# Two unused 96-byte tiles that move every large tile to a multiple of 128 bytes in its partition

## The chip, the core and the metric

The kernel runs on one core of one Trainium2 chip. A core has a matrix engine (TensorE, in the profile PE for the matrix multiplications and PEld for the loads of their stationary operand), VectorE (DVE), ScalarE (ACT), GpSimd (POOL), a queue engine that issues transfers (SP), and 16 DMA engines. They share an on-chip memory (SBUF) of 128 partitions; a tile has the same byte address in each of its partitions. TensorE writes its sums to another memory, PSUM, of 8 banks. The metric is the device time of one execution in microseconds; lower is better. Before the change the median of three runs is 2217.54 us (2216.56 to 2222.09).

## The reference

Three parts follow each other. `B, H, S, D` is 4, 8, 768, 48; the token matrix is 3072 by 384.

```python
for t in range(S):                                   # delta rule, 32 heads
    kt, vt, bt = k_n[:, :, t], v[:, :, t], beta[:, :, t, None]
    y[:, :, t] = einsum('bhd,bhde->bhe', q[:, :, t], state)
    v_old = einsum('bhde,bhd->bhe', state, kt)
    state = state + bt * einsum('bhd,bhe->bhde', kt, vt - v_old)
x = y.transpose(0, 2, 1, 3).reshape(3072, 384)
P = exp(x @ w_gate - max)                            # 8 experts
for _ in range(8):
    P /= P.sum(1) + 1e-9;  P /= P.sum(0) + 1e-9;  P *= N / E
out = sum(P[:, e] * (relu(x @ w1[e]) @ w2[e]) for e in range(8))   # 384 -> 1024 -> 384
a, b = out @ m2_w1, out @ m2_w2                      # 384 -> 1024, twice
return ((a * b) @ w3) @ w_out                        # 1024 -> 1024 -> 384
```

## The kernel before, in words

All large matrix products are done in the type fp32r, with each operand split in a high and a low part, so one product is three matmuls: high times high, high times low, low times high. A matmul loads a 128 x 128 stationary operand (its weights, read from SBUF by PEld) and streams a moving operand of 128 partitions by 512, 384 or 256 columns from SBUF past it. In the profile a matmul is written `b<-x,y`: `b` is a PSUM bank, `x` and `y` its two SBUF operands in alphabetical order, so the name alone doesn't say which of them moves; this section does.

Stage 1, until about 510 us, is the attention, in 12 chunks (`prep_k`, `invert`, `tt_make`, `prep_q`, `seq`), with expert 0 beside it (`e0`): there the moving operand is `xr` or `hA`, the weights are slots of `wA`, and a matmul has 256 columns.

Stage 2, 510 to 1878 us, is experts 1 to 7 (`unit`, line 975 on), in three passes over the tokens, with two halves of each expert: 42 units. A unit first computes the hidden layer: the weights are in `wA` or `wS`, the moving operand is one of nine token forms, of which three are in `xr` and six in `xT`, 512 columns. ScalarE and VectorE put relu of the result, split in high and low, into one of nine slots, seven in `hB` and two in `hA`. The second half of the unit has these slots as its moving operand, again 512 columns, and its weights in `wA`: six sums of 12 matmuls each. VectorE scales each sum (`tmp`), and GpSimd adds it to `acc`. Weights of the next unit come from DRAM by two large DMAs a pair (`load_pair`); VectorE, ScalarE and GpSimd also convert the last layer's weights there (`convert`).

Stage 3, from 1878 us (`phase_c`), first multiplies `w3` by `w_out` (384 columns, moving `wA`, weights `wS`), then takes the tokens in six chunks of 512. Each chunk has 144 matmuls of 512 columns, whose weights are in `xT` and whose moving operand is the split token chunk. That chunk lies in `xr` or in `wS`, by turns (`x2`, with the same code for both); then 96 matmuls of 384 columns follow with the weights in `hB` and `hA` and the moving operand in `wA`.

The order of all instructions is fixed when the kernel is built: a planner (`Plan.order`) takes each operation's priority and assumed cost and simulates the engines. Addresses don't enter it.

SBUF tiles are given out by `open`, which opens a pool on the left (low addresses, growing up) or on the right (high addresses, growing down) and places its tiles one after the other, each rounded up to 32 bytes. Pools close in the order of a stack, and what is opened later takes over their place. In the built program of the kernel before, the first tile `ones` is at byte 16,512 of a partition; `masks` (300 bytes) and `p` (900 bytes) leave the pool `const` at no multiple of 128, `wg` has 192 bytes, and `wA` starts at byte 18,720, which is 146 x 128 + 32. All that follows on the left (`hA` 67,872; `xr` 76,064; `yr`; the tiles of `seq`; `xst`; later `xT` 91,424 and `acc` 140,576) has a size that is a multiple of 128 and so also lies at 32 past a multiple of 128. The right side ends at byte 229,344, which is 1791 x 128 + 96; its tiles (those of `prep`, later `ident`, `rawB`, `hB` 177,632, `wS` 206,304, `cv`, `cvr`, `rt`, `pb`, `tmp`) have sizes that are multiples of 128 too and all lie at 96 past one. The two sides are thus 64 bytes apart, counted within 128. Taken within 512 bytes the left is at 288 and the right at 480. No tile of either side that holds an operand of a matmul with 384 or 512 columns starts at a multiple of 64.

Of the kernel before, what the change touches and what calls it, by code (L numbers as in the profile page):

```python
# [6 lines left out]
F32 = mybir.dt.float32  # L7
F32R = mybir.dt.float32r
# [13 lines left out]
NE = 8  # L22
# [288 lines left out]
class Kernel:  # L311
# [56 lines left out]
    def setup(self):  # L368
        nc, T, g = self.nc, self.T, self.g
        n = NCH * NG  # L370
        self.open("const", "left", ones=((128, 128), F32), masks=((128, 75), F32),
                  wgr=((128, 3, NE), F32), p=((128, NTT + 1, NE + 1), F32),
                  rs=((128, NTT), F32), cs=((128, NE), F32), sml=((128, 8), F32))
        self.open("wg", "left", wg=((128, 3, 2 * NE), F32R))
        self.open("wA", "left", wA=((128, EB, 1536), F32R))
        self.open("hA", "left", hA=((128, HA, 1024), F32R))
        self.open("xr", "left", xr=((128, 2, 2, 2, 3, 128), F32R))
        self.open("yr", "left", yr=((128, 3, 256), F32))
        self.open("seq", "left",
                  kraw=((128, NKR, NG, D), F32), kt=((128, NKT, NG, 64), F32), qt=((128, NQ, NG, 64), F32),  # L380
                  pt=((128, NPT, 2, 8, 64), F32), tt=((128, NTC, 2, 8, 64), F32), vs=((128, NV, NG, D), F32),
                  st=((128, NSU, NG, D), F32), u=((128, NSU, NG, D), F32),
                  bm=((128, n), F32), nv=((128, n), F32), nrm=((128, 3, 32), F32))
        self.open("xst", "left", xst=((128, NY, 2, 512), F32))
        self.open("prep", "right",
                  g12=((128, NG12, 2, NG, 32), F32), a0=((128, NA0, 32, 32), F32),
                  asys=((128, 1056), F32), t=((128, 1056), F32), prod=((128, NP, 1024), F32), xs=((128, 256), F32),
                  sq=((128, NG, D), F32), wraw=((128, 768), F32))
        self.open("dram", "left", space=DRAM, xs_d=((NCH, 2, DM, 128), F32), y0_d=((3, 128, NT), F32), p_d=((NE, NT), F32), xf_d=((4, 128, 3, 512), F32),
                  w1_d=((2, 128, 3, 1024), F32), w2_d=((2, 128, 3, 1024), F32), wo_d=((2, 128, 8, DM), F32),  # L390
                  w3_d=((2, 128, 8, 1024), F32),
                  wq_d=((NE, 4, 128, 3072), F32), ws_d=((NE, 4, 128, 1024), F32))
        cm = self.tc.tile_pool(name="psum", bufs=1, space=PSUM)
        pp = cm.__enter__()
        self.pools["psum"] = cm
        self.bank = [pp.tile([128, 512], F32, tag=f"b{i}", name=f"b{i}") for i in range(8)]
        self.psum = Ring(range(8), caps={"attn": 3, "eh": 1, "ey": 2, "hx": 6, "yb": 2, "h": 4, "y": 4})
        a = self.a
        for i, (nm, src) in enumerate((("masks", "masks"), ("bm", "beta"))):
            self.dma(lambda nm=nm: T[nm], lambda src=src: a[src], 65536, [], [nm], -20.05 + i * .1)  # L400
        g.op({"POOL": 1.75}, lambda e: nc.gpsimd.memset(T["t"], 0.0), w=["t"], prio=-5)
        g.op({"POOL": .2}, lambda e: nc.gpsimd.memset(T["t"].rearrange("p (i x) -> p i x", x=33)[:, :, 0:1], 1.0), w=["t"], prio=-5)
        self.dma(lambda: T["wgr"], lambda: a["moe_w_gate"].rearrange("(k p) e -> p k e", p=128), 12288, [], ["wgr"], -5)
        g.op({"POOL": .2}, lambda e: nc.gpsimd.memset(T["ones"], 1.0), w=["ones"], prio=-9)
        g.op({"POOL": .3}, lambda e: nc.gpsimd.memset(T["p"][:, :, NE:], 1e-9), w=["eps"], prio=30)
        g.op({"POOL": .2}, lambda e: nc.gpsimd.memset(T["p"][:, NTT:, 0:NE], 1e-9 / 128), w=["eps"], prio=30)
        g.op({"POOL": .2}, lambda e: nc.gpsimd.memset(T["asys"][:, 1024:], 0.0), w=["as2"], prio=-9)
        g.op({"DVE": .1}, lambda e: nc.vector.tensor_copy(T["wg"][:, :, 0:NE], T["wgr"]), r=["wgr"], w=["wgh"], prio=40)
        g.op({"DVE": .1}, lambda e: self.tt("DVE", T["wg"][:, :, NE:], T["wgr"], T["wg"][:, :, 0:NE].bitcast(F32),
                                           ALU.subtract), r=["wgr", "wgh"], w=["wg"], prio=40)  # L410
        self.kring = Ring(range(NKT), fifo=True)
        self.kraw = Ring(range(NKR), fifo=True)
        self.sring = Ring(range(NSU), fifo=True)
        self.uring = Ring(range(NSU), fifo=True)
        self.qring = Ring(range(NQ), fifo=True)
        self.vring = Ring(range(NV), fifo=True)
        self.ptring = Ring(range(2 * NPT), fifo=True)
        self.ttring = Ring(range(NTC), fifo=True)
        self.pring = Ring(range(NP))
        self.sqring = Ring(range(1))  # L420
        self.wraw = Ring(range(2))
        self.aring = Ring(range(NA0), fifo=True)
        self.yring = Ring(range(NY), fifo=True)
        self.y0ring = Ring([])
        self.xring = Ring(range(2), fifo=True)
        self.hring = Ring(range(HA))
        self.K, self.KR, self.S, self.Q, self.PT, self.TT, self.X, self.a0 = {}, {}, {}, {}, {}, {}, {}, {}
        self.SX = None
# [1025 lines left out]
```

## Time and profile before

| | |
|---|---|
| median of 3 runs | 2217.54 us |
| lowest and highest of them | 2216.56, 2222.09 us |
| span of the profiled execution | 2214.5 us |
| TensorE matmuls, busy | 2123.1 us, 96% |
| TensorE weight loads, busy | 1813.1 us, 82% |
| VectorE, GpSimd, ScalarE | 1247.8, 834.1, 722.1 us |
| mean granted TensorE clock | 0.976 |

The span runs from the first to the last instruction of the profiled execution; for that execution no time around it is given, so it is set against the median of the runs, which is 3.0 us more. Matmuls overlap each other, since one is still draining while the next streams; a row's duration of one matmul is therefore longer than the time from its start to the next one's start, which is what a matmul costs. The timeline merges equal matmuls into one row with their count, so the cost of one is the difference between the start of a row and the start of the next, divided by the count.

### The profile page before, as it was taken

Reading aid. Unit: us, or ns where it says so; the run is one execution under the profiler, and the core shown is the slowest. Engines: PE = TensorE matmul, PEld = TensorE weight load, DVE = VectorE, ACT = ScalarE, POOL = GpSimd, SP = SyncE. Lnnn points to the kernel's source line nnn. Section 1 sums busy time; section 2 is a strip of 40 time slices with the busy share of each in tenths; the row PEclk is TensorE's granted clock in tenths of the full one; section 3 lists DMA queues with packets and bytes.
Section 4 is the critical chain, followed back from the end, with each engine's and each line's share of the span. In section 5 each row is a group of like instructions: output and inputs, shape, how many; then the busy total and the mean of one; then the engine's idle time right before and its main releaser. Section 6 shows DMA issues by size and latency. Waiting matters only on the chain.

```text
span 2214.5 us, 39074 instructions
## 1 busy us (share of the span) xinstructions
PE 2123.1 (96%) x16017; PEld 1813.1 (82%) x16017; DVE 1247.8 (56%) x1958; ACT 722.1 (33%) x1384; POOL 834.1 (38%) x895
## 2 busy tenths in 40 slices
PE   2999999989999999999999999999999999999999
PEld 2899999987788778778887788788877888988888
DVE  7558666754445555576666766766667644222222
ACT  3333333334344244333233323323322322222222
POOL 3000000025666767753555544534456443300000
PEclk6889999999999999999999999999999999999999
DMA  5221331136565555675556545645564545600000
GB/s 196 88 79 50 104 95 48 31 81 216 206 218 176 179 190 201 224 262 203 194 174 231 187 148 196 216 162 197 205 212 166 201 157 159 135 29 29 15 15 29
DMA packets 163731, 326.86 MB, mean 148 GB/s; under 512 B 13088, under 2 KB 117472, under 8 KB 152032
## 3 DMA queue, kind: packets, MB, share of 16 engines
q1 hardware_dynamic: 129664, 189.10, 25.8%
q0 software_dynamic: 33888, 135.28, 18.1%
q8 instruction: 125, 2.05, 0.4%
q14 instruction: 54, 0.44, 0.1%
HBM read 230.38 MB, written 93.95 MB: 146 GB/s over the span
## 4 chain that ended last, share of the span: by engine, by line
PE 85%; DVE 6%; DMA 4%; ACT 2%; issue 2%; POOL 1%; SPq 0%; DVEq 0%; ACTq 0%; POOLq 0%
PE b L333 85%; DMA rawB<-in_moe_w 1%; DVE prod L344 1%; DMA xs_d<-xst 1%; DMA kraw<-in_k 1%; DMA xst<-xs_d 1%; DVE b L344 0%; DMA wA<-wq_d 0%; DVE cv L347 0%; ACT g L337 0%; DVE t L540 0%; DVE xr L344 0%; POOL acc L344 0%; POOL rawB L344 0%; POOL wA L344 0%
## 5 line engine op out<-in xcount | busy, mean ns | idle before, releaser
L333 PE MATMUL b<-hB,wA 128*128 128x512 f32 x2277 | 582.0, 396 | 0.1
L333 PEld LDWEIGHTS b<-hB,wA 128*128 128x128 f32 x2277 | 429.0, 188 | 104.0 <-ACT hB L1025 0.6
L344 POOL TENSOR_TENSOR acc<-acc,tmp 128x512 f32<-128x512 f32 x252 | 332.7, 1321 | 169.6 <-DVE tmp L344 166.5
L333 PE MATMUL b<-hA,wA 128*128 128x256 f32 (+1 forms) x1611 | 326.3, 335 | 7.5 <-DVE hA L347 7.5
L333 PE MATMUL b<-xr,wA 128*128 128x256 f32 (+1 forms) x1620 | 321.9, 336 | 0.0
L344 DVE TENSOR_TENSOR tmp<-b,pb 128x512 f32<-128x512 f32 x234 | 161.3, 690 | 234.6 <-PE b L333 219.8
L333 PEld LDWEIGHTS b<-hA,wA 128*128 128x128 f32 x1611 | 247.8, 190 | 42.6 <-DVE hA L347 9.4
L333 PEld LDWEIGHTS b<-xr,wA 128*128 128x128 f32 x1620 | 251.8, 192 | 31.5
L337 ACT ACTIVATE rt<-b 128x512 f32<-128x512 f32 x300 | 178.4, 598 | 262.4 <-PE b L333 256.0
L333 PE MATMUL b<-xT,wA 128*128 128x512 f32 x1008 | 252.6, 391 | 0.5 <-DMA wA<-wq_d 0.5
L344 DVE TENSOR_TENSOR b<-b,rt 128x512 f32<-128x512 f32 x252 | 174.2, 696 | 112.9 <-ACT rt L337 69.9
L333 PEld LDWEIGHTS b<-xT,wA 128*128 128x128 f32 x1008 | 189.8, 189 | 41.9 <-DMA wA<-wq_d 1.0
L333 PE MATMUL b<-xT,wS 128*128 128x512 f32 x756 | 202.8, 393 | 7.6 <-ACT rt L337 5.3
L344 POOL TENSOR_TENSOR cv<-cv 128x256 f32<-128x256 f32 (+2 forms) x177 | 129.4, 731 | 190.9 <-DVE cv L1215 111.9
L347 DVE SCALAR_TENSOR_TENSOR hB<-b,hB 128x512 fp32r<-128x512 f32 x253 | 172.6, 686 | 48.6 <-ACT hB L1025 47.7
L1025 ACT ACTIVATE hB<-b 128x512 fp32r<-128x512 f32 x253 | 150.3, 597 | 121.8 <-DVE b L344 96.1
L333 PEld LDWEIGHTS b<-xT,wS 128*128 128x128 f32 x756 | 141.1, 188 | 42.8 <-ACT rt L337 7.0
L344 DVE TENSOR_TENSOR rt<-b,rt 128x512 f32<-128x512 f32 x48 | 33.2, 692 | 188.8 <-PE b L333 188.8
L344 POOL TENSOR_TENSOR wA<-rawB,wA 128x768 fp32r<-128x768 f32 (+2 forms) x73 | 101.6, 1399 | 90.9 <-ACT wA L337 89.7
L337 ACT ACTIVATE cv<-cv 128x256 fp32r<-128x256 f32 x72 | 29.1, 405 | 268.8 <-DVE cv L347 268.8
L347 DVE SCALAR_TENSOR_TENSOR hA<-b,hA 128x512 fp32r<-128x512 f32 x131 | 90.2, 689 | 46.4 <-ACT hA L1025 27.3
L344 POOL TENSOR_TENSOR tt<-a,bm 128x256 f32<-128x256 f32 x7 | 5.3, 759 | 264.5 <-DVE a L576 113.0
(164 smaller groups left out, 2637.4 us busy)
## 6 DMA issues: line engine op xcount, KB each, us to landing
wA<-wq_d POOLq DMA_DIRECT2D x56, 1536.0 KB, 8.8
wq_d<-wA SPq DMA_DIRECT2D x28, 1536.0 KB, 7.2
wS<-ws_d POOLq DMA_DIRECT2D x56, 512.0 KB, 4.9
rawB<-in_moe_w SPq DMA_DIRECT2D x112, 192.0 KB, 4.2
ws_d<-wS SPq DMA_DIRECT2D x28, 512.0 KB, 3.0
w_d<-cv SPq DMA_DIRECT2D x112, 128.0 KB, 2.2
pb<-p_d SPq DMA_DIRECT2D x42, 256.0 KB, 4.5
cvr<-in_w3T SPq DMA_DIRECT2D x32, 256.0 KB, 3.3
```

The costliest lines, as they stand in the source:

```text
L333: self.nc.tensor.matmul(*args, skip_group_check=True, **kw)
L337: self.nc.scalar.activation(out=out, in_=in_, func=AF.Copy, **({} if scale is None else {"scale": scale}))
L344: self.E[eng].tensor_tensor(out=out, in0=in0, in1=in1, op=op)
L347: self.nc.vector.scalar_tensor_tensor(out=out, in0=in0, scalar=scalar, in1=in1, op0=op0, op1=op1)
L1025: g.op({"ACT": actb(512)}, lambda e: nc.scalar.activation(out=hv(0), in_=self.ps(s, 512), func=AF.Relu), r=[s], w=[(out, 0, 0)], prio=pe)
```

## The change

Two tiles that nothing reads or writes are opened, each with 24 elements of 4 bytes in a partition: `padl` at the end of the pool `wg`, right before `wA`, and `padr` in a pool of its own, `edge`, at the very end of the right side. No instruction, transfer, priority or cost changes. The left side then continues at 18,720 + 96 = 18,816 = 147 x 128, and the right side ends at 229,344 - 96 = 229,248 = 1791 x 128. Within 512 bytes both are at 384. The tiles ahead of `padl` (`ones`, `masks`, `wgr`, `p`, `rs`, `cs`, `sml`, `wg`) stay where they are.

```diff
-        self.open("wg", "left", wg=((128, 3, 2 * NE), F32R))
+        self.open("wg", "left", wg=((128, 3, 2 * NE), F32R), padl=((128, 24), F32))
         self.open("wA", "left", wA=((128, EB, 1536), F32R))
...
         self.open("xst", "left", xst=((128, NY, 2, 512), F32))
+        self.open("edge", "right", padr=((128, 24), F32))
         self.open("prep", "right",
```

## Rows read from the trace of the kernel before

**Rows 1.** The page: busy time by engine, and the chain of waits by engine.

```profile
span 2214.5 us, 39074 instructions
...
PE 2123.1 (96%) x16017; PEld 1813.1 (82%) x16017; DVE 1247.8 (56%) x1958; ACT 722.1 (33%) x1384; POOL 834.1 (38%) x895
...
PE 85%; DVE 6%; DMA 4%; ACT 2%; issue 2%; POOL 1%; SPq 0%; DVEq 0%; ACTq 0%; POOLq 0%
```

**Rows 2.** Windows by stage: bounds and length, busy us and count, clock, DMA.

```profile
0.00:510.00 510.00, 444.20 (x8601) 430.01 (x8601) 342.64 (x560) 174.89 (x367) 54.69 (x52) 0.91 0.28 87
510.00:1878.00 1368.00, 1346.52 (x5788) 1087.79 (x5787) 827.70 (x1294) 465.44 (x885) 749.30 (x813) 1.00 0.57 196
1878.00:1944.00 66.00, 66.00 (x336) 60.10 (x336) 16.44 (x24) 14.53 (x24) 20.70 (x28) 1.00 0.62 124
1944.00:2214.00 270.00, 266.34 (x1297) 235.16 (x1295) 61.02 (x82) 67.20 (x109) 9.39 (x4) 1.00 0.07 24
```

**Rows 3.** Chain of waits by line: window 0 to 510, 510 to 1878, 1878 to 2214.

```profile
by line: PE b L333 69.5%; issue 3.0%; DVE prod L344 2.8%; DMA xs_d<-xst 2.6%; DMA kraw<-in_k 2.4%; DMA xst<-xs_d 2.3%; ACT g L337 1.6%; DVE t L540 1.4%; DMA kt<-in_kT 1.2%; DVE tt L344 1.0%; DVE xs L540 1.0%; DVE asys L574 0.7%; ACT tt L337
...
by line: PE b L333 87.7%; DMA rawB<-in_moe_w 2.1%; issue 1.6%; DVE b L344 0.7%; DMA wA<-wq_d 0.6%; DVE cv L347 0.6%; POOL acc L344 0.5%; POOL rawB L344 0.5%; POOL wA L344 0.4%; DVE tmp L344 0.4%; DVE rawB L344 0.3%; POOL cv L344 0.3%; DVE x
...
by line: PE b L333 98.9%; ACT tmp L337 0.1%; issue 0.0%
```

**Rows 4.** Timeline of PE, stage 3: start, us until the last one's end, operands, count.

```profile
1960.59 33.76 PE L333 MATMUL b<-wS,xT 128*128 128x512 f32 x144
1994.18 4.33 PE L333 MATMUL b<-wA,hB 128*128 128x384 f32 x24
...
2010.88 32.84 PE L333 MATMUL b<-xr,xT 128*128 128x512 f32 x144
2043.56 6.41 PE L333 MATMUL b<-wA,hB 128*128 128x384 f32 x36
2049.80 2.27 PE L333 MATMUL b<-wA,hA 128*128 128x384 f32 x12
2051.91 6.41 PE L333 MATMUL b<-wA,hB 128*128 128x384 f32 x36
```

**Rows 5.** Timeline of PE in one unit of stage 2.

```profile
1052.99 2.26 PE L333 MATMUL b<-hB,wA 128*128 128x512 f32 x9
1055.09 0.85 PE L333 MATMUL b<-hA,wA 128*128 128x512 f32 x3
1055.78 2.26 PE L333 MATMUL b<-hB,wA 128*128 128x512 f32 x9
...
1071.76 1.54 PE L333 MATMUL b<-xT,wS 128*128 128x512 f32 x6
1073.13 0.84 PE L333 MATMUL b<-xr,wA 128*128 128x512 f32 x3
...
1079.29 1.52 PE L333 MATMUL b<-xr,wA 128*128 128x512 f32 x6
1080.65 0.84 PE L333 MATMUL b<-xT,wA 128*128 128x512 f32 x3
```

**Rows 6.** Matmul groups, shapes apart: count, busy us (union), mean ns of one.

```profile
L333 PE MATMUL b<-hB,wA 128*128 128x512 f32 x2277 | 582.0, 396 | 0.1
L333 PE MATMUL b<-xT,wA 128*128 128x512 f32 x1008 | 252.6, 391 | 0.5 <-DMA wA<-wq_d 0.5
L333 PE MATMUL b<-hA,wA 128*128 128x512 f32 x747 | 214.0, 393 | 7.5 <-DVE hA L347 7.5
L333 PE MATMUL b<-xr,wA 128*128 128x512 f32 x756 | 207.7, 392 | 0.0
L333 PE MATMUL b<-xT,wS 128*128 128x512 f32 x756 | 202.8, 393 | 7.6 <-ACT rt L337 5.3 <-ACT wS L337 2.1
L333 PE MATMUL b<-xr,wA 128*128 128x256 f32 x864 | 114.2, 287 | 0.0
L333 PE MATMUL b<-hA,wA 128*128 128x256 f32 x864 | 112.3, 285 | 0.0
L333 PE MATMUL b<-wS,xT 128*128 128x512 f32 x432 | 101.3, 395 | 0.0
L333 PE MATMUL b<-xr,xT 128*128 128x512 f32 x432 | 99.9, 390 | 0.0
L333 PE MATMUL b<-xr,wS 128*128 128x512 f32 x252 | 67.0, 395 | 5.7 <-ACT rt L337 5.6
```

**Rows 7.** Weight loads beside matmuls in that unit, timeline of PEld.

```profile
1052.99 1.82 PEld L333 LDWEIGHTS b<-hB,wA 128*128 128x128 f32 x8
1054.86 0.65 PEld L333 LDWEIGHTS b<-hA,wA 128*128 128x128 f32 x3
```

**Rows 8.** Instructions by tile: duration ns min/median/max, first and last start.

```profile
L333 PE MATMUL b<-hB,wA x2277: 388/394/628, 525.0 to 1877.4; 128*128 128x512 f32 x190
...
L333 PE MATMUL b<-xT,wA x1008: 387/389/628, 500.5 to 1860.7; 128*128 128x512 f32 x168
L333 PE MATMUL b<-xT,wS x756: 388/392/505, 509.5 to 1857.3; 128*128 128x512 f32 x189
L333 PE MATMUL b<-xr,xT x432: 387/389/402, 1883.9 to 2143.0; 128*128 128x512 f32 x144
L333 PE MATMUL b<-wS,xT x432: 388/395/398, 1960.6 to 2193.3; 128*128 128x512 f32 x144
```

**Rows 9.** DMA issues: KB each, median us from issue to landing.

```profile
wA<-wq_d POOLq DMA_DIRECT2D x56, 1536.0 KB, 8.8
```

## The prediction

> **What bounds the kernel now.** I read the page first: TensorE's matmuls are busy 96% of the span of 2214.5 us, and 85% of the chain of waits that ended last is PE [rows 1]. The windows by stage say where. In stage 2 PE is busy 1346.52 of 1368 us at a granted clock of 1.00 (the level of 2.4 GHz), VectorE 827.70 and GpSimd 749.30; in stage 3 PE is busy 66.00 of 66 and 266.34 of 270 us [rows 2]. The chain, cut by window, is PE for 69.5% of stage 1, 87.7% of stage 2 and 98.9% of stage 3 [rows 3]. So from 510 us on the kernel takes as long as its matmuls take, and a change without any new or removed instruction matters if it alters the time of one matmul. Then I looked for matmuls of one shape that differ in time, and whether the difference goes with addresses.
>
> It does. In stage 3 the same code runs 144 matmuls of 512 columns with the same weights (`xT`), once with the moving operand in `xr` and once in `wS`. With `xr` (left side, 32 past a multiple of 128) the run starts at 2010.88 and the next work at 2043.56: 32.68 us, 226.9 ns each. With `wS` (right side, 96 past) it is 1960.59 to 1994.18: 33.59 us, 233.3 ns each [rows 4]. The difference of 6.4 ns is the place of the moving operand and nothing else. Stage 2 repeats it: moving `hB` (right) nine take 2.10 us, 233.3 ns each; moving `xr` with weights `wA` (both left) six take 1.36 us, 226.7 ns; moving `hA` (left) between two runs of `hB` 0.69 us for three, 230.0 ns; moving `xT` with weights in `wS` (right) 1.37 us for six, 228.3 ns [rows 5]. Over all of a group, the medians order themselves alike: 389 ns where both operands are on the left, 392 with the weights on the right, 394 and 395 with the moving operand on the right [rows 8].
>
> **The change part by part.** The two tiles are never used, so they add no instruction, wait or transfer, and the planner, which knows no addresses, emits the same order. What is left is the shift: left tiles from 32 to 0, right tiles from 96 to 0 within 128 bytes. The two sides, 64 bytes apart now, become equal, also within 512 bytes, which is how the left tiles stand to each other today.
>
> I forecast that every 512-column matmul then runs as one with both operands on the left does now, at 226.9 ns. Two readings of the rows give that. Either what costs is where in a 128-byte piece a stream starts, and 32 bytes of the first piece (96 past) are worse than 96 (32 past), in which case a whole piece is no worse; or what costs is the 64-byte offset between the moving stream and the loads of the next weights, which start at the same instant (both rows begin at 1052.99) [rows 5, 7]. The terms, counts from [rows 6]:
> - moving `hB`: 2277 x (233.3 - 226.9) = 14.6 us, stage 2;
> - moving `hA`: 747 x (230.0 - 226.9) = 2.3 us, stage 2 (its neighbours in time are the `hB` runs);
> - weights in `wS`: 756 + 252 = 1008 matmuls; the timeline gives 1.4 ns each, the medians 392 - 389 = 3; I take 2, nearer to the timeline, which measures cost and not duration: 2.0 us (1.4 to 3.0);
> - moving `wS`: 432 x 6.4 = 2.8 us, stage 3.
>
> What gets through: in stage 2, 18.9 us x 0.877, the chain's share, = 16.6; in stage 3, 2.8 x 0.989 = 2.8. Together 19.4 us. The rest of stage 2's chain is waits for `rawB` (2.1%), `wA` (0.6%) and others; there a faster matmul only waits longer. A unit lasts 1368 / 42 = 32.6 us and would shorten by 0.45; the next unit's two large weight loads land 8.8 us after issue [rows 9], and VectorE and GpSimd have over a third of the stage free, so nothing is late next by so small a step. Were it all hidden by those, stage 3's 2.8 us would remain.
>
> Matmuls of 384 columns I leave as they are: with weights in `hB` 36 take 6.24 us, 173.3 ns each, which is 13.3 ns over their 160 ns at 2.4 GHz, just as the clean 512-column one is 13.6 over 213.3 [rows 4]; those with weights in `hA` take 2.11 / 12 = 175.8, but 132 x 2.5 ns is only 0.3 us. Those of 256 columns have both operands on the left [rows 6], and I take 0 for them as well.
>
> The other engines and the DMAs also read and write at new addresses, and no row shows them at a phase other than today's. The largest effect of a phase that any row shows is 233.3 / 226.9, 2.8%. On the chain's shares of VectorE, DMA, ScalarE and GpSimd, 6 + 4 + 2 + 1 = 13% of 2214.5, this is 288 us x 2.8% = 8.1 us, in either direction [rows 1]. I take 0, since these shares are many small pieces that would not all move the same way, and keep both ends.
>
> For the transfers a rule speaks against the change. The Trainium skill, DMA: Bandwidth & Descriptors, section How a descriptor splits into AXI transactions, says that a read which doesn't start at a multiple of 256 bytes also fetches the bytes back to that multiple. By it, as an estimate, a row of 3072 bytes of the left side would go from 97 beats of 32 bytes to 100, as 128 past the multiple is further than 32, and one of the right side from 103 to 100; on the 8.5% of stage 1's chain that are DMA waits [rows 3], 43 us, 3% would be 1.3 us, and the sum 18.1 instead of 19.4. No row shows it, and the sum above does without it.
>
> So the span would go from 2214.5 to 2195.1 and the median, 3.0 us above the span, from 2217.54 to **2198**.
>
> **The rivals.** First, no change: it isn't the phase but the place. `hB` and `wS` are the operands above byte 177,000, the left ones lie below 141,000, and each side has one phase only, so the rows can't part place and phase. For it speaks that `hA`, with the left's own phase, still shows 230.0 [rows 5]; against it, that high weights cost far less than high moving operands, and at 384 columns nothing [rows 4, 8]. It gives 2217, give or take the few us of other engines. The Trainium skill, TensorE: Matmul & The Clock Gate, Part 2, Step-by-step, says that TensorE has two independent read ports, so that loading the next weights takes no bandwidth from the running matmul. By that rule the offset between two streams would be harmless, and of my two readings only the first would be left, or this rival; the trace so far shows a loss beside such loads but not that they cause it.
>
> Second, slower: equal phase is the bad case. If the moving stream and the weight load that starts with it meet in the same piece of memory when both start a piece, then every 512-column matmul pays what `hB` pays now. Price: 756 + 1008 clean ones of stage 2 x 6.4 = 11.3 us, `hA` 747 x 3.3 = 2.5, weights in `wS` 1008 x 4.4 = 4.4, together 18.2 x 0.877 = 16.0; stage 3's 432 x 6.4 x 0.989 = 2.7. That is 18.7 us, 2236. It decides if a 512-column matmul at phase 0 loses more than 3.3 ns on average, which is today's excess: 14.6 + 2.3 + 2.0 + 2.8 = 21.7 us over the 6660 of [rows 6]. For it: something in the phase costs, and 0 is untried. Against: left-left pairs have equal phase now and are the fast ones.
>
> Third, much faster: the 13.6 ns that even a clean matmul takes over 512 columns at 2.4 GHz is also a start at no whole piece, and goes. 6660 x 13.6 = 91 us more, so some 2108. Against it: the 256 columns of `xr` are read in two runs of 128, those of `hA` in one, and they take 287 and 285 ns [rows 6]; a loss by start would come twice.
>
> Fourth, the tiles don't shift anything, because a tile without use gets no room, or something else lands ahead. But `sml` has no use either, and `wg` lies 32 bytes past the end of `cs`, where `sml` would be. 2217.5.
>
> **How the numbers follow.** Forecast 0.60, place 0.22, slower 0.11, much faster 0.04, no shift 0.03. What a measurement of this kernel can tell from no change is about 0.3%, 6.7 us (its three runs span 5.5). Faster by more than that is 0.60 + 0.04 = 0.64, within it 0.22 + 0.03 = 0.25, slower 0.11. The forecast's own range takes from 2198 the part of the saving that I counted as hidden (2.3 us), the open 0.9 of the weights in `wS` and the 8.1 of other engines, 2187; upwards it adds the 8.1 and 0.5 of `wS`, 2207. The range reaches up to the no-change cases with some room, 2222; the slower and much faster ones, 0.15, stay outside.
>
> **What would show it.** Right: the stage 3 runs of 144 with `wS,xT` take 32.7 us like those with `xr,xT`; medians of all 512-column groups meet at 389 ns; a unit is 0.4 to 0.45 us shorter; the counts of instructions are equal. Place: `wS,xT` stays at 33.6. Collision: `xr,xT` rises to 33.6. Much faster: 144 take below 31.5. If the matmuls gain and the time doesn't, PE's share of stage 2's chain falls below 87%, and waits for `rawB` or `wA` grow. The prediction is wrong if the two runs of 144 still differ, or if both moved.

## The result and the profile after

The changed kernel takes 2197.12 us (median of 4 runs, 2196.03 to 2198.37), where the kernel before took 2219.82 beside it (4 runs, 2216.56 to 2222.95): a ratio of 0.9906, 95% interval 0.9889 to 0.9923. It is faster: by 22.7 us by these medians, by 20.9 by that ratio, which is not the quotient of the two medians (0.9898). The forecast was 2198, which is the 2217.54 known then less a saving of 19.4 us.

The page of the changed kernel: span, busy time by engine, and the chain of waits by engine [rows 1].

```profile
span 2196.6 us, 39074 instructions
...
PE 2102.4 (96%) x16017; PEld 1815.7 (83%) x16017; DVE 1244.6 (57%) x1958; ACT 720.4 (33%) x1384; POOL 832.7 (38%) x895
...
PE 80%; DVE 6%; DMA 5%; POOL 3%; issue 2%; ACT 2%; SPq 1%; DVEq 0%; POOLq 0%; ACTq 0%
```

Every count is the same as before; matmul busy time fell by 20.7 us, the span by 17.9, and no other engine's busy time moved by more than 3.2. The span fell by less than the medians did: the profile of the changed kernel comes from the slowest of its four runs (2198.37), while the run of the profile before is not known. What became shorter is the single matmul. First the timeline of PE in stage 3, against [rows 4]:

```profile
1945.61 32.84 PE L333 MATMUL b<-wS,xT 128*128 128x512 f32 x144
1978.29 4.35 PE L333 MATMUL b<-wA,hB 128*128 128x384 f32 x24
...
1994.95 32.84 PE L333 MATMUL b<-xr,xT 128*128 128x512 f32 x144
2027.63 6.43 PE L333 MATMUL b<-wA,hB 128*128 128x384 f32 x36
```

Both runs of 144 now last 32.68 us, 226.9 ns a matmul; the one with `wS` took 33.59. The timeline of PE in a unit of stage 2, against [rows 5]:

```profile
1047.50 2.20 PE L333 MATMUL b<-hB,wA 128*128 128x512 f32 x9
1049.54 0.84 PE L333 MATMUL b<-hA,wA 128*128 128x512 f32 x3
1050.22 2.20 PE L333 MATMUL b<-hB,wA 128*128 128x512 f32 x9
...
1065.86 1.52 PE L333 MATMUL b<-xT,wS 128*128 128x512 f32 x6
1067.22 0.84 PE L333 MATMUL b<-xr,wA 128*128 128x512 f32 x3
...
1073.34 1.52 PE L333 MATMUL b<-xr,wA 128*128 128x512 f32 x6
1074.70 0.84 PE L333 MATMUL b<-xT,wA 128*128 128x512 f32 x3
```

Nine with `hB` take 2.04 us (226.7 ns each), three with `hA` 0.68 (226.7), six with weights in `wS` 1.36 (226.7), six of `xr` with `wA` 1.36 as before. The groups by tile, duration ns min/median/max and first and last start, say it for all of them [rows 8]:

```profile
L333 PE MATMUL b<-hB,wA x2277: 387/389/629, 526.0 to 1862.3; 128*128 128x512 f32 x190
...
L333 PE MATMUL b<-xT,wA x1008: 388/389/566, 501.2 to 1845.9; 128*128 128x512 f32 x168
L333 PE MATMUL b<-xT,wS x756: 387/389/796, 510.3 to 1842.5; 128*128 128x512 f32 x189
L333 PE MATMUL b<-xr,xT x432: 387/389/398, 1868.8 to 2126.1; 128*128 128x512 f32 x144
L333 PE MATMUL b<-wS,xT x432: 387/389/398, 1945.6 to 2175.4; 128*128 128x512 f32 x144
```

All five medians are 389 ns. The starts also place the gain in these two profiles. From the first matmul of `xT` with `wA` to the last one of `hB` it was 500.5 to 1877.4 and is 501.2 to 1862.3: stage 2 lost 15.8 us. From there to the end of the span it was 337.1 and is 334.3: stage 3 lost 2.8. Stage 1 lost nothing (0.7 us more).

The chain of waits by line, of stage 2 and of stage 3 [rows 3]; then that of stage 2 from a second profile of the same kernel, taken with the last experiments below:

```profile
by line: PE b L333 78.6%; DMA rawB<-in_moe_w 4.2%; issue 2.4%; POOL wA L344 1.4%; POOL acc L344 1.3%; POOL rawB L344 1.2%; DVE cv L347 1.1%; SPq L364 1.0%; DVE b L344 0.9%; POOL wS L344 0.8%; DMA wA<-wq_d 0.6%; DMA cvr<-in_moe_w 0.6%; DVE r
...
by line: PE b L333 98.7%; ACT tmp L337 0.1%; issue 0.0%
...
by line: PE b L333 85.6%; DMA rawB<-in_moe_w 2.2%; issue 1.5%; DVE cv L347 1.2%; DVE b L344 0.9%; DMA w_d<-cv 0.8%; DMA wA<-wq_d 0.6%; DVE hB L347 0.5%; POOL acc L344 0.5%; POOL rawB L344 0.5%; DVE tmp L344 0.4%; DVE cv L1216 0.4%; POOL cv 
```

In the first profile PE's share of stage 2's chain is 78.6%, against 87.7 before, and the wait for raw weights (`rawB`) 4.2% against 2.1. In the second they are 85.6 and 2.2%, at nearly the same time (2197.76 us against 2198.37). So these shares swing by as much between two executions of one kernel, and no shift of the chain in stage 2 is shown. The large weight loads land in 9.1 us in the first profile and in 8.9 in the second, against 8.8 before [rows 9].

### The profile page after: what moved, and what is told of

It reads as the page before. It is cut to its first block, busy times and chain, and to the rows that moved or that the text cites. A ratio compares the mean times of both kernels' runs of the same rounds, so it can differ in the third digit from the quotient of the medians.

```text
span 2196.6 us, 39074 instructions
## 1 busy us (share of the span) xinstructions
PE 2102.4 (96%) x16017; PEld 1815.7 (83%) x16017; DVE 1244.6 (57%) x1958; ACT 720.4 (33%) x1384; POOL 832.7 (38%) x895
## 4 chain that ended last, share of the span: by engine, by line
PE 80%; DVE 6%; DMA 5%; POOL 3%; issue 2%; ACT 2%; SPq 1%; DVEq 0%; POOLq 0%; ACTq 0%
PE b L333 80%; DMA rawB<-in_moe_w 3%; POOL wA L344 1%; POOL acc L344 1%; SPq L364 1%; POOL rawB L344 1%; DVE cv L347 1%; DVE prod L344 1%; DVE b L344 1%; DMA xst<-xs_d 1%; POOL wS L344 0%; DMA xs_d<-xst 0%; DMA wA<-wq_d 0%; DMA cvr<-in_moe_w 0%; DVE rawB L344 0%
## 5 line engine op out<-in xcount | busy, mean ns | idle before, releaser
L333 PE MATMUL b<-hB,wA 128*128 128x512 f32 x2277 | 566.8, 391 | 0.0
```

The source lines that it names most:

```text
L333: self.nc.tensor.matmul(*args, skip_group_check=True, **kw)
```

## The experiments

The result bears out the forecast but not yet its reason. The prediction had two readings: a bad start of a stream within 128 bytes, or an offset between the moving operand and the weights. The expectations call them theory A and theory B. The rival by place is theory C; D says that both operands must be at multiples of 128; E came after the first four runs. The kernels differ from the kernel before or the changed one in unused tiles alone and compute the same. In the names, "left" and "right" are followed by the starts within 128 bytes, in the later ones within 512. Each ratio is to the kernel before on the same chip.

**Both sides at 96, moving the left by 64 bytes.**

```diff
-        self.open("wg", "left", wg=((128, 3, 2 * NE), F32R))
+        self.open("wg", "left", wg=((128, 3, 2 * NE), F32R), padl=((128, 16), F32))
```

> Only the left side is moved, by 64 bytes: both sides then lie at 96 past a multiple of 128 and are equal to each other, though no tile is at a multiple of 128. Theory A (the start of the moving stream within 128 bytes costs, and 96 is the bad start): all 6660 matmuls of 512 columns run at 233.3 ns, a run of 144 takes 33.6 us with either moving operand, and the time is about 2236 us. Theory B (the offset between the moving stream and the weights read beside it costs, and equal is free): all at 226.7 to 226.9 ns, 32.7 us for both runs of 144, about 2197 us as in the changed kernel. Theory C (the place in memory, high addresses are slow): as before the change, 32.7 us with xr and 33.6 with wS, about 2218; the changed kernel has already spoken against C.

Measured: 2219.21 us, ratio 1.0019 (0.9998 to 1.0041). Timeline of PE in stage 3 of this kernel:

```profile
1961.53 33.62 PE L333 MATMUL b<-wS,xT 128*128 128x512 f32 x144
1994.99 4.39 PE L333 MATMUL b<-wA,hB 128*128 128x384 f32 x24
...
2011.85 32.85 PE L333 MATMUL b<-xr,xT 128*128 128x512 f32 x144
2044.53 6.51 PE L333 MATMUL b<-wA,hB 128*128 128x384 f32 x36
2050.88 2.25 PE L333 MATMUL b<-wA,hA 128*128 128x384 f32 x12
```

33.46 us with `wS` moving, 232.4 ns each, while the 144 with `xr` take 32.68 us as before. Theory A is refuted: `xr` now starts at 96 and is clean, that is, without the excess. Theory B, with a period of 128, is refuted as well: the sides are equal within 128 and the excess remains.

**Both sides at 32, moving the right by 64 bytes.**

```diff
+        self.open("edge", "right", padr=((128, 16), F32))
         self.open("prep", "right",
```

> Only the right side is moved, by 64 bytes: both sides lie at 32 past a multiple of 128. Theory A: 32 was a good start for the left tiles, so it is one for the right tiles, all at 226.9 ns, about 2197 us. Theory B: the sides are equal, all at 226.9 ns, about 2197 us. Multiples of 128 are then not needed. If they were (theory D: only whole pieces are clean and the left tiles of before were clean for another reason), the run of 144 with wS stays above 33 us and the time above 2205.

Measured: 2219.6 us, ratio 1.0014 (0.9997 to 1.0030). A miss for A and B alike: 32 is no good start in itself. In durations this kernel is a copy of the one with both at 96, as the group of `hB` with `wA` shows, first there and then here:

```profile
L333 PE MATMUL b<-hB,wA 128*128 128x512 f32 x2277 | 577.3, 395 | 0.0
...
L333 PE MATMUL b<-hB,wA 128*128 128x512 f32 x2277 | 577.7, 395 | 0.2 <-ACT hB L1026 0.2
```

Theory D was left, and C.

**Half of the change: the left side alone, then the right side alone.**

```diff
-        self.open("wg", "left", wg=((128, 3, 2 * NE), F32R))
+        self.open("wg", "left", wg=((128, 3, 2 * NE), F32R), padl=((128, 24), F32))
```

> Half of the change: only the left tiles go to multiples of 128, the right tiles stay at 96 past. Theory A: what moves from the right side still starts badly, 233.3 ns for hB and for wS as moving operand, 33.6 us for that run of 144, hA near 230, and no gain: 2216 to 2220 us. Theory B: the sides are now 32 bytes apart instead of 64 within 128; not equal, so a part of the excess remains, between 226.9 and 233.3 ns, 2200 to 2218 us.

```diff
+        self.open("edge", "right", padr=((128, 24), F32))
         self.open("prep", "right",
```

> The other half: only the right tiles go to multiples of 128, the left ones stay at 32 past. Theory A: 32 and 0 are both good starts, so every matmul is clean, 226.9 ns, 32.7 us for both runs of 144, about 2197 us, the whole gain by one tile. Theory B: the sides are 32 bytes apart, not equal, and what mixes the sides (hB with wA, xT with wS, wS with xT) keeps a part of the excess: between 226.9 and 233.3 ns, 2200 to 2218 us.

Measured: 2226.14 us, ratio 1.0045 (1.0022 to 1.0068), for the left tile alone and 2224.99, ratio 1.0036 (1.0018 to 1.0055), for the right one alone. Either half makes the kernel slower; the change only works whole. Both expectations for the time were too low. Groups with shapes apart (count, busy us, mean ns), first of the left tile alone, then of the right one alone:

```profile
L333 PE MATMUL b<-hB,wA 128*128 128x512 f32 x2277 | 583.8, 398 | 0.0
L333 PE MATMUL b<-hA,wA 128*128 128x512 f32 x747 | 216.0, 397 | 7.3 <-DVE hA L347 7.3
L333 PE MATMUL b<-xT,wS 128*128 128x512 f32 x756 | 206.7, 398 | 6.8 <-ACT rt L337 4.2 <-ACT wS L337 2.4
```

```profile
L333 PE MATMUL b<-hB,wA 128*128 128x512 f32 x2277 | 584.5, 398 | 0.0
```

398 for `hB` was 396 before [rows 6], and weights in `wS` rose from 393 to 398. The two halves have nothing in common but the distance between the sides. That pattern is theory E: right minus left, within 256 bytes, is 192 before, 96 in both halves, 128 in both kernels that are equal within 128, and 0 in the changed kernel, whose sides I had made equal within 512 without asking for it. These kernels, where they have one distance, agree in their means within 2 ns.

**Equal sides without alignment.**

```diff
+        self.open("edge", "right", padr=((128, 48), F32))
         self.open("prep", "right",
```

> Only one tile, of 192 bytes, at the end of the right side: the left stays at 288 within 512 bytes, 32 past a multiple of 128, and the right comes to 288 too. No large tile is at a multiple of 64. Theory E (a 512-column matmul is free of the excess when its moving operand and its weights start at the same place within a period of 256 or 512 bytes, wherever that is): all groups at 389 ns, both runs of 144 at 32.7 us, 2195 to 2199 us, the whole gain of the change without any alignment. Theory D (both must be at multiples of 128): like the four kernels before, 33.6 us with wS, 2214 to 2222 us.

Measured: 2196.71 us, ratio 0.9907 (0.9873 to 0.9941). Timeline of PE in stage 3 of this kernel:

```profile
1946.05 32.84 PE L333 MATMUL b<-wS,xT 128*128 128x512 f32 x144
1978.73 4.35 PE L333 MATMUL b<-wA,hB 128*128 128x384 f32 x24
...
1995.40 32.84 PE L333 MATMUL b<-xr,xT 128*128 128x512 f32 x144
2028.08 2.09 PE L333 MATMUL b<-wA,hB 128*128 128x384 f32 x11
```

The whole gain of the change, with every large tile 32 bytes past a multiple of 128. Theory D falls: multiples of 128 are not what helps.

**Alignment without equal sides.**

```diff
-        self.open("wg", "left", wg=((128, 3, 2 * NE), F32R))
+        self.open("wg", "left", wg=((128, 3, 2 * NE), F32R), padl=((128, 56), F32))
...
+        self.open("edge", "right", padr=((128, 24), F32))
         self.open("prep", "right",
```

> All large tiles at multiples of 128, but the left at 0 and the right at 384 within 512 bytes. Theory D: as good as the change, 2195 to 2199 us, both runs of 144 at 32.7 us. Theory E: the sides are 128 bytes apart, as in the kernels with both sides at 32 and with both at 96 past a multiple of 128; 33.6 us with wS as moving operand, weights in wS at a median of 391 to 393 ns, 2215 to 2222 us.

Measured: 2215.87 us, ratio 0.9996 (0.9977 to 1.0014): all large tiles at multiples of 128, and no gain. Timeline of PE in stage 3, then two groups with shapes apart, of this kernel:

```profile
1955.58 33.62 PE L333 MATMUL b<-wS,xT 128*128 128x512 f32 x144
1989.04 4.39 PE L333 MATMUL b<-wA,hB 128*128 128x384 f32 x24
```

```profile
L333 PE MATMUL b<-hB,wA 128*128 128x512 f32 x2277 | 577.3, 395 | 0.0
L333 PE MATMUL b<-xT,wS 128*128 128x512 f32 x756 | 205.9, 397 | 7.5 <-ACT rt L337 5.0 <-ACT wS L337 2.2
```

33.46 us for the run with `wS`, and means as in the two other kernels with a distance of 128 (the median of `xT` with `wS` is 395 ns, a little above the 391 to 393 expected). This pair of runs decides between alignment and distance.

**The period: multiples of 256, the sides 256 bytes apart within 512.**

```diff
-        self.open("wg", "left", wg=((128, 3, 2 * NE), F32R))
+        self.open("wg", "left", wg=((128, 3, 2 * NE), F32R), padl=((128, 56), F32))
...
+        self.open("edge", "right", padr=((128, 56), F32))
         self.open("prep", "right",
```

> All large tiles at multiples of 256: the left at 0 and the right at 256 within 512 bytes. Theory D: as good as the change, 2195 to 2199 us. Theory E with a period of 256: clean as well, 32.7 us for both runs of 144. Theory E with a period of 512: 256 bytes apart, an excess remains, the run with wS above 33 us and 2205 to 2222 us.

Measured: 2193.82 us, ratio 0.9891 (0.9857 to 0.9926), clean. Timeline of PE in stage 3:

```profile
1941.97 32.84 PE L333 MATMUL b<-wS,xT 128*128 128x512 f32 x144
1974.65 2.61 PE L333 MATMUL b<-wA,hB 128*128 128x384 f32 x14
```

So two starts that differ by 256 count as equal, and the period is not 512. It is not 128 or a part of it either, since sides 128 apart are not clean.

**Equal or not, on the same side.** The left tile of the change stands behind `wA` instead of ahead of it.

```diff
-        self.open("wg", "left", wg=((128, 3, 2 * NE), F32R), padl=((128, 24), F32))
-        self.open("wA", "left", wA=((128, EB, 1536), F32R))
+        self.open("wg", "left", wg=((128, 3, 2 * NE), F32R))
+        self.open("wA", "left", wA=((128, EB, 1536), F32R), padl=((128, 24), F32))
```

> The two tiles of the change, but the left one stands behind wA instead of ahead of it: wA stays at 288 within 512 bytes and every other large tile is at 384, the right ones too. Theory E: what pairs tiles other than wA is clean (xr with xT and wS with xT, 32.7 us for 144), and what has its weights in wA gets the excess of tiles 96 bytes apart, now also xr and xT with wA, which are both on the left and were nearly clean in every kernel so far: medians 391 to 395 ns for all four groups with wA. That is some 4700 of the 6660 matmuls at about 7 ns, 33 us, so 2217 to 2228 us. Theory C (high addresses are slow) and any theory by sides: xr and xT with wA stay at 389 ns. Theory D: xr with wA suffers, by the weights, and so does hB.

Measured: 2225.71 us, ratio 1.0037 (1.0017 to 1.0056). Timeline of PE in stage 3 and in a unit of stage 2, then groups with shapes apart, all of this kernel:

```profile
1968.44 32.85 PE L333 MATMUL b<-wS,xT 128*128 128x512 f32 x144
2001.12 4.33 PE L333 MATMUL b<-wA,hB 128*128 128x384 f32 x24
...
1071.69 1.55 PE L333 MATMUL b<-xT,wS 128*128 128x512 f32 x6
1073.08 0.86 PE L333 MATMUL b<-xr,wA 128*128 128x512 f32 x3
...
1079.36 1.56 PE L333 MATMUL b<-xr,wA 128*128 128x512 f32 x6
1080.76 0.86 PE L333 MATMUL b<-xT,wA 128*128 128x512 f32 x3
```

```profile
L333 PE MATMUL b<-xT,wA 128*128 128x512 f32 x1008 | 257.3, 395 | 2.0 <-DMA wA<-wq_d 2.0
L333 PE MATMUL b<-xr,wA 128*128 128x512 f32 x756 | 210.6, 396 | 0.0
L333 PE MATMUL b<-xT,wS 128*128 128x512 f32 x756 | 205.6, 397 | 6.4 <-ACT rt L337 3.9 <-ACT wS L337 2.3
```

`wS` moving past `xT`, from the right against the left, is clean (32.68 us for 144), and `xr` past `wA`, both on the left, costs 1.40 us for six, 233.3 ns each, instead of 226.7. Low or high, left or right, doesn't matter: theory C is refuted and E holds. One thing I had not expected: `xT` with weights in `wS`, equal in this kernel, has a mean of 397 and takes 1.39 us for six, 231.7 ns, between matmuls with `wA`. So matmuls with equal starts can be slow when unequal ones stand around them; what passes from one to the other the runs don't show.

**The terms of the sum, one by one.** Starting from the kernel before, one unused tile between `hB` and `wS` makes `hB` equal to the left side and leaves `wS`; two tiles make `wS` equal and leave `hB`.

```diff
-            self.open("hBp", "right", hB=((128, HB, 1024), F32R), wS=((128, 4, 1024), F32R))
+            self.open("hBp", "right", hB=((128, HB, 1024), F32R), padh=((128, 48), F32), wS=((128, 4, 1024), F32R))
```

> An unused tile of 192 bytes between hB and wS, without the change: hB (and what lies below it) comes to the left side's place within 256 bytes, wS stays 192 bytes off. By the sum of the prediction the terms of hB and hA go, 14.6 + 2.3 us of matmul time, and those of wS stay: 14.8 us less on the chain, about 2203 us; hB with wA at a median of 389 ns, the run of 144 with wS still 33.6 us. If the excess also sticks to matmuls that follow an unequal pair, hA is clean but xr and xT with wA, between weights in wS, stay a little above.

```diff
-            self.open("hBp", "right", hB=((128, HB, 1024), F32R), wS=((128, 4, 1024), F32R))
+            self.open("hBp", "right", hB=((128, HB, 1024), F32R), padh=((128, 16), F32), wS=((128, 4, 1024), F32R), pads=((128, 48), F32))
```

> The counterpart: wS comes to the left side's place within 256 bytes, hB and what lies below it stay 192 bytes off. By the sum the terms of wS go, 2.8 us in stage 3 and 2.0 in stage 2: about 2213 us; both runs of 144 at 32.7 us, xT with wS at 389 ns, hB with wA still at 394 and hA at its 393 mean.

> The changed kernel once more, beside the one with all large tiles at multiples of 256 bytes. Theory E says that the two are equal in every matmul, 2194 to 2200 us each.

> All large tiles at multiples of 256 bytes. It came out 3 us below the kernel with both sides at 288 on the same chip, which is within the spread of either. Theory E: the same as the changed kernel within 0.2%. If transfers or other engines gain by 256 bytes, 3 us less than the changed kernel.

All four ran beside each other and beside the kernel before, at 2216.63 us. Measured: `hB` alone 2202.53 us, ratio 0.9941 (0.9916 to 0.9966); `wS` alone 2210.31, ratio 0.9965 (0.9941 to 0.9988); the changed kernel 2196.27, ratio 0.9913 (0.9889 to 0.9936); multiples of 256 2194.97, ratio 0.9910 (0.9889 to 0.9930). By medians that is 14.1 and 6.3 us for the parts, 20.4 together, and 20.4 for the change; that the sums meet so exactly is chance, since each of the intervals is 10 us wide or more. Groups with shapes apart, first with `hB` alone equal, then with `wS` alone equal:

```profile
L333 PE MATMUL b<-hB,wA 128*128 128x512 f32 x2277 | 567.0, 390 | 0.3 <-ACT hB L1025 0.3
L333 PE MATMUL b<-hA,wA 128*128 128x512 f32 x747 | 212.0, 391 | 5.9 <-DVE hA L347 5.9
L333 PE MATMUL b<-wS,xT 128*128 128x512 f32 x432 | 101.3, 395 | 0.0
```

```profile
L333 PE MATMUL b<-hB,wA 128*128 128x512 f32 x2277 | 582.3, 397 | 0.0
L333 PE MATMUL b<-hA,wA 128*128 128x512 f32 x747 | 214.9, 395 | 7.5 <-DVE hA L347 7.5
L333 PE MATMUL b<-wS,xT 128*128 128x512 f32 x432 | 98.5, 389 | 0.0
```

`hA` never changed its place in either, and it is at 391 when `hB` is equal and at 395 when it is not: its excess comes and goes with that of its neighbours. The expectation that `xr` and `xT` with `wA` would stay above in the first of the two was a miss; `xT` with `wA` has a median of 389 there. Multiples of 256 are no better than the change: the 3 us of the earlier run were spread, and no version here beats the changed kernel.

## Why the prediction was right

What bounds the kernel: right. The gain came from TensorE's matmuls (20.7 us of busy time) and in stages 2 and 3, in which PE was most of the chain; stage 1 gained nothing.

The terms: moving `hB` was put at 6.4 ns each and lost 6.6 by the timeline (233.3 to 226.7); `hA` 3.1, lost 3.3; moving `wS` 6.4, lost 6.3; weights in `wS` 2 ns, where the timeline row lost 1.6 (228.3 to 226.7) and the medians 3. No row has the cost of all of these, but it can be worked out from the single starts in the two traces, leaving out gaps above 300 ns: `xT` with `wS` went from 229.4 to 227.1 ns on average and `xr` with `wS` from 229.2 to 227.3, so 2 was right. `hB` and `hA` without `wS` were forecast to bring 14.8 us and brought 14.1 by medians; `wS` alone 4.6 to 4.8, and brought 6.3; the interval of its ratio stands for 2.7 to 13.1 us of 2216.63, so the two can't be told apart.

What gets through: 16.6 us were expected in stage 2 and 15.8 came in the first profile; between the same two starts the second profile of the changed kernel has 17.0 less than before. In stage 3 2.8 were expected, and 2.8 and 2.7 came. That a part of stage 2's saving is lost to other waits is not shown: over the profiles of all kernels with equal starts stage 2 is 13.9 to 18.9 us shorter than in the one profile of the kernel before, and this range holds both 16.6 and the full 18.9. Nor do waits for `rawB` bear it out, which doubled in one profile of the changed kernel and stayed as they were in the other. My test by the chain was a bad one: I wrote that PE's share would fall below 87% if the matmuls gained and the time didn't. It is 78.6 and 85.6% in two profiles of a kernel that did gain, and 84.7 and 86.2% in the two kernels with both sides at 96 and at 32, which gained nothing.

The other engines and DMAs, taken at 0 within 8.1 us either way: right within what the runs can tell. The rule of the Trainium skill (DMA: Bandwidth & Descriptors, How a descriptor splits into AXI transactions) would make starts at multiples of 256 bytes the cheapest ones; the kernel that has them is equal to the changed one, 2194.97 against 2196.27 with intervals that nearly coincide, so its effect is too small to be seen here.

Where the reasoning failed: the two readings from which the forecast was drawn. The first, a bad start within 128 bytes, is wrong. The second, an offset between the moving operand and the weights, is right in that the offset counts, but I took its period for 128 bytes, since the sides stood 64 apart in it. That the forecast held is in this part luck: the changed tiles happen to be equal within 512 too, which I noted only in passing. With the left tile 128 bytes further, as in the kernel with 0 and 384, the same argument would have forecast the same gain and been wrong. The kernel before could have warned me: two distances, 64 and 192 within 256, have costs as different as 2 and 6.4 ns, and a period of 128 makes both 64. One row was also cut short: the eight loads of [rows 7] are the last of nine, since that view began at 1053. The whole row, from a wider window, is

```profile
1052.76 2.05 PEld L333 LDWEIGHTS b<-hB,wA 128*128 128x128 f32 x9
```

and begins with the matmul ahead of the run. So what starts with a matmul is the load of the next one's weights, as the prediction says.

The rivals: no change by place is refuted by the tile behind `wA`, and tiles that shift nothing by the gain itself. Slower by equal phase is refuted; equal is the good case. Much faster is refuted: at every start tried a matmul keeps at least 226.7 ns, which is 13.4 over the 213.3 of 512 columns at 2.4 GHz. The Trainium skill, TensorE: Matmul & The Clock Gate, Part 2, Step-by-step, has the weight loads take nothing from the running matmul, because of two read ports. The runs show a loss that this rule does not foresee: the time of a matmul depends on where its two operands lie to each other, 6.6 ns of 226.7 for `hB` in the kernel before. That the load beside it takes these ns is not shown.

What stays open is the mechanism. The distance within 256 bytes decides; that the two reads meet in the same piece of the memory is only argued. Nor do the runs part a matmul's own weights from those being loaded beside it, since both come from the same tile nearly always. Nor is the order in which matmuls are slowed explained: in the kernel before, of three matmuls with `hA` between two runs of `hB` the first takes 227.2 ns on average, the second 232.5 and the third 230.9, again worked out from the single starts.

## What to carry to other kernels

When matmuls of one shape differ by a few ns and their tiles are different ones, compare the start addresses of the moving and the stationary operand: here the difference of the two within 256 bytes decided, not the alignment of either. An unused tile costs room but no instruction, and moves a whole side, but each half of such a shift has to be judged by the distances it makes; half of this change was slower than none. And when a forecast rests on two readings that give the same number, ask which nearby kernel would part them, since the time alone won't.

## What the runs showed of the hardware that was not expected

- A fp32r matmul of 512 columns takes 226.7 ns where the starts of its two SBUF operands are equal within 256 bytes. It takes 233.3 with `hB` moving at a distance of 192 and 232.4 for `wS` moving at 128, in the runs shown; at 96 it is 233.3 for `xr` in the kernel with the tile behind `wA`. The two halves of the change, also at 96, have the largest mean of `hB` with `wA`, 398 ns against 391 in the changed kernel; with the tile behind `wA` it is 396, so the distance alone doesn't fix the size of the loss.
- The direction can count too: in the kernel before, the right side's operand cost 6.4 ns when it moved, 192 bytes past its weights, and about 2 when it held the weights, which is a distance of 64. With the left tile alone (96 and 160) both groups have a mean of 398 ns.
- Matmuls of 384 columns have their own distances: before, at 64, 36 with weights in `hB` take 6.24 us, 173.3 ns each [rows 4]; at 128 they take 6.35 us, 176.4 ns each (2044.53 to 2050.88 in the kernel with both sides at 96).
- Matmuls with equal starts can be slow close to unequal ones: 231.7 ns instead of 226.7 for `xT` with `wS` between matmuls with `wA`, while a run of 144 equal ones keeps 226.9 on average. It is not so always: with `hB` alone equal, `xT` with `wA` stays at a median of 389 ns between matmuls with weights in `wS`.
